# Expert products three steps apart, and three PSUM banks that change owner when the last transform ends

## The chip, the cores and the metric

One Trainium2 chip, one core of it. The metric is device time in microseconds (us) of one execution. The kernel before takes 2305.79 us, the median of three runs (2302.34 to 2326.87).

## The reference, cut to what matters

The input x has 8 sequences of 5696 tokens with 128 features. Every feature column is convolved causally with its own filter h (an FFT of twice the length, a product, the inverse FFT, the first 5696 outputs). The 45568 result rows then go through a mixture of eight experts, each token through one of them:

```
logits = y @ w_gate + modality_bias[modality_id];  e = argmax(logits);  g = softmax(logits)[e]
out[token] = g * (relu(y @ w1[e]) @ w2[e])          # w1: 128 x 1024, w2: 1024 x 128
```

All of it is float32. The kernel splits each factor of the expert products into a high and a low part and adds three products (high by high, low by high, high by low).

## The kernel before, in words

**Transform.** The convolution runs in stages with HBM between them: `stage1` and `stage23` for two groups of four sequences, then `stage4`, which ends the transform, computes the gate (logits, argmax, rank of each token in its expert) and sends each finished row by an indirect DMA of GpSimd to the region of its expert in HBM (`dispatch`, L298). The first 27 of 45 column blocks of `stage4` of the first group run beside `stage23` of the second group. All the rest of `stage4` runs beside the experts.

**Experts.** `Moe.run` works through 104 tiles in order: 81 tiles of 512 tokens and, at the end, 23 of 256 (`TSL`). A tile has eight steps, or four when it has 256 tokens. `gemm1` of step f multiplies one 128-wide slice of w1 with the tile's tokens (L567 to L569, three matmuls; six in a 256-token step, which does two slices), into one PSUM bank `ph`. ScalarE makes `hh`, the rectified high part (L572); VectorE then makes `hl`, the rest (L573), from `ph` and `hh`. `gemm2` of the same step takes `hh` and `hl` through a slice of w2 and adds into the bank `po` (L589 to L591; L589 needs only `hh`). It is issued `LAG` = 2 steps after `gemm1`.

Per tile there is also `load` (L535, the token rows by SP's queue, three tiles ahead), `load_weights` (L543, 2 MB into one of three slots, only where the expert of that slot changes), `prep` (L550, transposes of the tokens into a bank `pxt`, then `mxh` and `mxl`), and after the last `gemm2` the copy `ot` (L594), `finish` (L602, transposes back, into a bank of the same pool `pxt`; L605 scales by the gate) and `scatter` (L613, one indirect DMA of GpSimd per 128 tokens, one in each step). The calls hang on LAG: `load_weights` for tile t + 2 comes in step LAG - 1 of tile t, and `finish` of tile t - 1 in step LAG. `load` of tile t + 3 reuses the buffer of tile t - 2, so SP waits in it until the scatters of tile t - 2 have landed.

**PSUM.** There are eight banks: during the experts two for `ph`, two for `po`, one for `pxt`, and three for `stage4` (two `py`, one `pl`), held to the end of the kernel though `stage4` ends earlier.

**Order of the work.** SP's queue keeps the order in which the program issues. On the other engines a planner orders the instructions by a simulated timeline: each engine takes what is ready in the simulation, the earliest issued first. On the chip that order is fixed, and an engine that meets an instruction whose operands are not there waits. `run_all` (L712) issues steps of `rest()` (all that is left of the transform) and of `moe.run()` in turns.

Of the kernel before, what the change touches and what calls it, by code (L numbers as in the profile page):

```python
# [10 lines left out]
F32 = mybir.dt.float32  # L11
F32R = mybir.dt.float32r
# [13 lines left out]
TS = 512  # L26
# [39 lines left out]
def run_all(*gens):  # L66

    live = [[g, float(r), 0.0] for g, r in gens]
    while live:
        for it in list(live):  # L70
            it[2] += it[1]
            while it[2] >= 1.0:
                it[2] -= 1.0
                try:
                    next(it[0])
                except StopIteration:
                    live.remove(it)
                    break
# [3 lines left out]
def conv_moe(  # L82
# [436 lines left out]

    class Moe:  # L520
        def __init__(self, wp, sp, pst, psh, pso):
            self.sp, self.pst, self.psh, self.pso = sp, pst, psh, pso
            self.slots = [wp.tile([128, 2, 2, FF], F32R, name=f"slot{i}") for i in range(NSLOT)]
            self.st = {}
            self.outs = []
            self.tabs = {}

        def load(self, t):
            lv, j = JOBS[t]
# [15 lines left out]
        def prep(self, t):  # L545
            st = self.st[t]
            rt, ts, ns = st["rt"], st["ts"], st["ns"]
            px = self.pst.tile([128, NSUB, 128], F32, name="pxt")
            for c in range(ns):
                nc.tensor.transpose(px[:, c, :], rt[:, c, :D], ident)  # L550
            pf = px.rearrange("p c t -> p (c t)")[:, :ts]
            xh = self.sp.tile([128, TS], F32R, name="mxh")
            xl = self.sp.tile([128, TS], F32R, name="mxl")
            nc.scalar.copy(xh[:, :ts], pf)
            nc.vector.tensor_tensor(xl[:, :ts], pf, xh[:, :ts].bitcast(F32), op=ALU.subtract)
            st.update(xh=xh[:, :ts], xl=xl[:, :ts])

        def gemm1(self, t, f):
            w = self.slots[t % NSLOT]
            st = self.st[t]  # L560
            ts = st["ts"]
            n = TS // ts
            ph = self.psh.tile([128, TS], F32, name="ph")
            for i in range(n):
                fs = slice((f * n + i) * 128, (f * n + i + 1) * 128)
                po = ph[:, i * ts:(i + 1) * ts]
                nc.tensor.matmul(po, w[:, 0, 0, fs], st["xh"], start=True, stop=False)  # L567
                nc.tensor.matmul(po, w[:, 0, 0, fs], st["xl"], start=False, stop=False)  # L568
                nc.tensor.matmul(po, w[:, 0, 1, fs], st["xh"], start=False, stop=True)  # L569
            hh = self.sp.tile([128, TS], F32R, name="hh", bufs=4)  # L570
            hl = self.sp.tile([128, TS], F32R, name="hl", bufs=4)
            st["act"] = nc.scalar.activation(hh, ph, AF.Relu)  # L572
            nc.vector.scalar_tensor_tensor(hl, ph, 0.0, hh.bitcast(F32), op0=ALU.max, op1=ALU.subtract)  # L573
            st["h", f] = (hh, hl)
# [22 lines left out]
        def finish(self, t):  # L597
            st = self.st.pop(t)
            ns = st["ns"]
            pq = self.pst.tile([128, NSUB, 128], F32, name="pxt")  # L600
            for c in range(ns):
                nc.tensor.transpose(pq[:, c, :], st["ot"][:, c * 128:(c + 1) * 128], ident)  # L602
            of = self.sp.tile([128, NSUB, D], F32, name="of")
            rt = st["rt"]
            nc.vector.tensor_tensor(of[:, :ns], pq[:, :ns], rt[:, :ns, D:D + 1].to_broadcast([128, ns, D]), op=ALU.mult)  # L605
            ri = rt.bitcast(I32)
            for c in range(ns):
                self.outs.append((t, c, ri, of))
# [8 lines left out]
                    tc.add_manual_dep(d.ins, after.ins.name, PACED, reason="spacing")  # L617

        def run(self):
            LAG = 2  # L620
            total = len(JOBS)
            steps = []
            for t, (lv, j) in enumerate(JOBS):
                n = 4 if lv == len(LEVELS) - 1 else 8
                steps += [(t, f, n) for f in range(n)]
            self.load(0)
            self.load_weights(0)
            self.load(1)
            self.load_weights(1)
            self.load(2)  # L630
            self.prep(0)
            for g in range(len(steps) + LAG):
                t, f, n = steps[g] if g < len(steps) else (total, g - len(steps), 4)
                if f == 0 and t + 3 < total:
                    while JOBS[t + 3][0] not in self.tabs:
                        dispatch(4)
                        yield
                    self.load(t + 3)
                if t < total:
                    self.gemm1(t, f)  # L640
                    dispatch(1, self.st[t]["act"])
                    self.scatter(1, self.st[t]["act"])
                else:
                    self.scatter(1)
                if g >= LAG:
                    self.gemm2(*steps[g - LAG][:2])
                if f == LAG - 1 and t + 2 < total:
                    self.load_weights(t + 2)
                if t + 1 < total:
                    if f == (4 if n == 8 else 1):  # L650
                        self.prep(t + 1)
                if f == LAG and t >= 1:
                    self.finish(t - 1)
                yield
            if t < total or f < LAG:
                self.finish(total - 1)
            self.scatter(len(self.outs))
# [2 lines left out]
    ftab = fx.enter_context(tc.tile_pool(name="ftab", bufs=1, side="right")).tile([128, NQ, 2, 64], F32, name="ftab")  # L660
    with tc.tile_pool(name="s1a", bufs=2) as sp, tc.tile_pool(name="p1a", bufs=3, space=PSUM) as ps1:
        run_all((stage1(0, sp, ps1, ftab), 1))
    with tc.tile_pool(name="p4", bufs=2, space=PSUM) as ps4, \
            tc.tile_pool(name="p4l", bufs=1, space=PSUM) as ps4l:
        with tc.tile_pool(name="s2", bufs=2) as sp2, tc.tile_pool(name="p2x", bufs=3, space=PSUM) as psx, \
                tc.tile_pool(name="p2u", bufs=2, space=PSUM) as psu:
            with tc.tile_pool(name="s1b", bufs=2) as sp1:
                run_all((stage23(0, sp2, psx, psu), 3), (stage1(1, sp1, ps4, ftab), 2))
            fx.close()
            tp = ctx.enter_context(tc.tile_pool(name="table", bufs=1, side="right"))  # L670
            sp4 = ctx.enter_context(tc.tile_pool(name="s4", bufs=2, side="right"))
            with tc.tile_pool(name="ws", bufs=1) as wsp:
                run_all((stage23(1, sp2, psx, psu), 3), (stage4(0, sp4, ps4, ps4l, 0, QA, True), S4R), (presplit(wsp), 0.25))
            dispatch(len(queue))

        def fence():

            nc.gpsimd.dma_start(rows_d[E * REGION:E * REGION + TS, :].rearrange("(p c) w -> p c w", c=NSUB), padt)

        ev = [None] * (len(LEVELS) + 1)  # L680
        with tc.tile_pool(name="moew", bufs=1) as wp, tc.tile_pool(name="moe", bufs=2) as sp, \
                tc.tile_pool(name="pm1", bufs=1, space=PSUM) as pst, tc.tile_pool(name="pm3", bufs=2, space=PSUM) as psh, \
                tc.tile_pool(name="pm2", bufs=2, space=PSUM) as pso, tc.manual_schedule(engines={mybir.EngineType.SP}):
            moe = Moe(wp, sp, pst, psh, pso)

            def level(lv, src):
                tab, ev[lv] = table(tp, lv, ev[lv - 1])
                moe.tabs[lv] = (tab, src)

            s4 = stage4(0, sp4, ps4, ps4l, QA, NQ)  # L690
            for _ in range(AHEAD):
                next(s4)
            fence()
            level(0, views[NVIEW])

            def rest():
                yield from s4
                while queue:
                    yield
                fence()  # L700
                level(1, views[NVIEW])
                yield from stage4(1, sp4, ps4, ps4l, 0, NQ)
                while queue:
                    yield
                padrow = tp.tile([1, E], I32, name="padrow")
                nc.vector.tensor_copy(padrow, bases[0][0:1, :])
                for e in range(E):
                    r0 = nc.sync.value_load(padrow[0:1, e:e + 1], min_val=e * REGION, max_val=e * REGION + NTOK)
                    nc.sync.dma_start(rows_d[bass.ds(r0, TS), :].rearrange("(p c) w -> p c w", c=NSUB), padt)
                level(2, rows_d)  # L710
                level(3, rows_d)
            run_all((rest(), RATE), (moe.run(), 1))  # L712


# [81 lines left out]
```

## Time and profile before

| | |
|---|---|
| median of the runs shown | 2305.79 us |
| the profiled execution, its own time | 2318.76 us |
| its span, first to last instruction | 2317.0 us |
| TensorE (PE) busy | 2107.8 us, 91% |
| VectorE, ScalarE, GpSimd busy | 63%, 49%, 47% |
| mean granted clock of TensorE | 0.962 |

The span falls into stages: transform alone to about 870 us, transform and experts together to about 1595, experts alone with 512-token tiles to about 2130, with 256-token tiles to about 2305. Busy time of PE is modelled and short waits can be hidden in it, so the distance from the start of one matmul to the start of the next is read as well. The clock column is the share of full speed that the throttle granted.

### The profile page before, as it was taken

The page shows a single profiled execution, that of the slowest core. Times are in us where ns is not written, and L with a number is a line of the kernel's source. Part 1 is how long each engine was busy: PE and PEld are TensorE (multiplying, and loading weights), DVE is VectorE, ACT ScalarE, POOL GpSimd, SP SyncE. Part 2 cuts the span into 40 slices and gives each one's busy share as a digit, 9 for nine tenths or more (in the row PEclk, how much of TensorE's full clock was granted, in tenths as well). Part 3 has the DMA queues.
Part 4 walks back from the last instruction along what each step waited for, and adds up shares of the span by engine and source line. Part 5 has one row for each costly group of instructions (what it writes and reads, how often), then busy time and mean ns, then how long its engine had stood idle before and what let it go on. Part 6 is the DMA issues. An engine that isn't in the chain of part 4 may idle for free.

```text
span 2317.0 us, 33168 instructions
## 1 busy us (share of the span) xinstructions
PE 2107.8 (91%) x9598; PEld 1502.3 (65%) x9598; DVE 1466.0 (63%) x2473; ACT 1132.8 (49%) x2010; POOL 1085.6 (47%) x1050
## 2 busy tenths in 40 slices
PE   6779999899999897999899989889999999999997
PEld 5655555334444445777677667667888888888886
DVE  6559999776777984576465555555555555555443
ACT  6557776333333343555455555334444444444433
POOL 2126655344777763665665556553333333333222
PEclk9899999999999997999999999979999999999999
DMA  9999989899997765433244432132111121123331
GB/s 338 325 307 318 312 293 301 290 314 320 300 282 240 230 193 214 130 109 113 88 149 149 150 101 85 55 123 80 44 47 42 45 82 44 45 80 109 106 104 56
DMA packets 198309, 388.89 MB, mean 168 GB/s; under 512 B 32757, under 2 KB 63833, under 8 KB 193776
## 3 DMA queue, kind: packets, MB, share of 16 engines
q1 hardware_dynamic: 148832, 276.81, 36.5%
q10 hardware_dynamic: 25776, 62.34, 8.5%
q0 software_dynamic: 23520, 47.61, 6.2%
q8 instruction: 78, 1.28, 0.2%
q14 instruction: 103, 0.84, 0.1%
HBM read 393.95 MB, written 174.21 MB: 245 GB/s over the span
## 4 chain that ended last, share of the span: by engine, by line
PE 56%; issue 3%; ACT 2%; DVE 2%; another core or an unknown queue 2%; DMA 1%; POOL 1%; SPq 0%; POOLq 0%; ACTq 0%; DVEq 0%
PE ph L567 8%; PE ph L569 7%; PE po L589 7%; PE po L590 7%; PE po L591 7%; PE ph L568 7%; PE py L357 4%; PE pxt L602 2%; PE pxt L550 2%; PE py L364 1%; PE pl L371 1%; DVE hl L573 1%; ACT hh L572 1%; PE pu L239 1%
## 5 line engine op out<-in xcount | busy, mean ns | idle before, releaser
L573 DVE SCALAR_TENSOR_TENSOR hl<-ph,hh 128x512 fp32r<-128x512 f32 x740 | 506.7, 689 | 457.1 <-ACT hh L572 361.7
L572 ACT ACTIVATE hh<-ph 128x512 fp32r<-128x512 f32 x740 | 440.9, 599 | 600.0 <-PE ph L569 410.5
L613 POOL DMA_INDIRECT out<-of,mrt x370 | 363.1, 981 | 576.7 <-ACT hh L572 475.5
L298 POOL DMA_INDIRECT rows<-rt,idx x360 | 375.3, 1042 | 274.5 <-ACT hh L572 163.5
L271 POOL TENSOR_TENSOR t<-t,t 96x512 f32<-96x512 f32 x212 | 296.7, 1416 | 223.9 <-DVE t L264 214.4
L589 PE MATMUL po<-hh,slot 128*128 128x512 f32 (+1 forms) x832 | 328.3, 395 | 42.3 <-ACT hh L572 25.7
L264 DVE TENSOR_TENSOR t<-px,hs 96x512 f32<-96x512 f32 x512 | 318.2, 676 | 61.5 <-PE pu L239 17.4
L567 PE MATMUL ph<-mxh,slot 128*128 128x512 f32 (+1 forms) x832 | 331.1, 398 | 17.7 <-DVE hl L573 8.1
L590 PE MATMUL po<-hl,slot 128*128 128x512 f32 (+1 forms) x832 | 313.4, 377 | 0.1
L569 PE MATMUL ph<-mxh,slot 128*128 128x512 f32 (+1 forms) x832 | 312.1, 375 | 0.8 <-issue 0.8
L568 PE MATMUL ph<-mxl,slot 128*128 128x512 f32 (+1 forms) x832 | 312.7, 376 | 0.0
L591 PE MATMUL po<-hh,slot 128*128 128x512 f32 (+1 forms) x832 | 310.6, 373 | 0.0
L261 PE MATMUL px<-z,m 96*96 96x512 f32 x512 | 261.5, 610 | 11.1 <-DVE t L264 5.8
L589 PEld LDWEIGHTS po<-hh,slot 128*128 128x128 f32 x832 | 159.3, 192 | 82.4 <-ACT hh L572 36.5
L244 ACT COPY ut<-pu 90x512 f32<-90x512 f32 x256 | 145.0, 583 | 132.6 <-PE pu L239 60.3
L239 PE MATMUL pu<-t,mi 96*96 96x512 f32 x352 | 182.9, 625 | 20.7 <-ACT ut L244 11.4
L567 PEld LDWEIGHTS ph<-mxh,slot 128*128 128x128 f32 x832 | 159.7, 192 | 53.9 <-DVE hl L573 18.5
L590 PEld LDWEIGHTS po<-hl,slot 128*128 128x128 f32 x832 | 158.8, 191 | 35.5 <-DVE hl L573 2.7
L569 PEld LDWEIGHTS ph<-mxh,slot 128*128 128x128 f32 x832 | 159.1, 191 | 31.4 <-issue 0.5
L591 PEld LDWEIGHTS po<-hh,slot 128*128 128x128 f32 x832 | 158.7, 191 | 30.0
L568 PEld LDWEIGHTS ph<-mxl,slot 128*128 128x128 f32 x832 | 159.9, 192 | 23.6 <-issue 0.5
L261 PEld LDWEIGHTS px<-z,m 96*96 96x96 f32 x512 | 82.2, 166 | 115.4 <-issue 64.3
(157 smaller groups left out, 2892.2 us busy)
## 6 DMA issues: line engine op xcount, KB each, us to landing
slot<-w12s SPq DMA_DIRECT2D x104, 2048.0 KB
z<-z SPq DMA_DIRECT2D x256, 180.0 KB
z<-z SPq DMA_DIRECT2D x90, 320.0 KB
z<-z SPq DMA_DIRECT2D x90, 256.0 KB
ua<-ut SPq DMA_DIRECT2D x128, 180.0 KB
ub<-ut SPq DMA_DIRECT2D x128, 180.0 KB
mrt<-rows SPq DMA_DIRECT2D x81, 260.0 KB
w12s<-ws ACTq DMA_DIRECT2D x16, 1024.0 KB
```

Of the source, the lines that this page charges most:

```text
L261: nc.tensor.matmul(px[:KP], mm, zbuf[i][k % NZ], start=True, stop=True)
L264: nc.vector.tensor_tensor(prod[i, j].rearrange("p (b d) -> p b d", d=D), px[:KP].rearrange("p (b d) -> p b d", d=D), hs[:, j, k % KH].unsq ...
L298: d = nc.gpsimd.indirect_dma_start(views[count[0] % NVIEW], bass.IndirectOffsetOnAxis(ap=idx[:, t:t + 1], axis=0), rt[:, t, :], None, boun ...
L567: nc.tensor.matmul(po, w[:, 0, 0, fs], st["xh"], start=True, stop=False)
L568: nc.tensor.matmul(po, w[:, 0, 0, fs], st["xl"], start=False, stop=False)
L569: nc.tensor.matmul(po, w[:, 0, 1, fs], st["xh"], start=False, stop=True)
L572: st["act"] = nc.scalar.activation(hh, ph, AF.Relu)
L573: nc.vector.scalar_tensor_tensor(hl, ph, 0.0, hh.bitcast(F32), op0=ALU.max, op1=ALU.subtract)
L589: nc.tensor.matmul(po, w[:, 1, 0, fs], hh[:, cs], start=k == 0, stop=False)
L590: nc.tensor.matmul(po, w[:, 1, 0, fs], hl[:, cs], start=False, stop=False)
L591: nc.tensor.matmul(po, w[:, 1, 1, fs], hh[:, cs], start=False, stop=k == 7)
L613: d = nc.gpsimd.indirect_dma_start(oviews[(t * NSUB + c) % NVIEW], bass.IndirectOffsetOnAxis(ap=ri[:, c, D + 1:D + 2], axis=0), of[:, c, : ...
```

## The change

`LAG` goes from 2 to 3: `gemm2` is issued three steps after `gemm1`, and the calls that hang on LAG move one step later. `hh` and `hl` have five buffers instead of four. The PSUM pools of `stage4` move to the other end of PSUM, so that they can be closed alone. They are closed when `rest()` has issued its last work, and the three banks go to two new pools: from then on `ph` takes turns through four banks and `pxt` through two.

```diff
     class Moe:
         def __init__(self, wp, sp, pst, psh, pso):
-            self.sp, self.pst, self.psh, self.pso = sp, pst, psh, pso
+            self.sp, self.pst, self.psh, self.pso = sp, [pst], [psh] * 2, pso
+            self.n = [0, 0]
...
+        def bank(self, i, shape, name):
+            pools = (self.pst, self.psh)[i]
+            self.n[i] += 1
+            return pools[self.n[i] % len(pools)].tile(shape, F32, name=name)
...
-            px = self.pst.tile([128, NSUB, 128], F32, name="pxt")
+            px = self.bank(0, [128, NSUB, 128], "pxt")
...
-            ph = self.psh.tile([128, TS], F32, name="ph")
+            ph = self.bank(1, [128, TS], "ph")
...
-            hh = self.sp.tile([128, TS], F32R, name="hh", bufs=4)
-            hl = self.sp.tile([128, TS], F32R, name="hl", bufs=4)
+            hh = self.sp.tile([128, TS], F32R, name="hh", bufs=5)
+            hl = self.sp.tile([128, TS], F32R, name="hl", bufs=5)
...
-            pq = self.pst.tile([128, NSUB, 128], F32, name="pxt")
+            pq = self.bank(0, [128, NSUB, 128], "pxt")
...
-            LAG = 2
+            LAG = 3
...
-    with tc.tile_pool(name="p4", bufs=2, space=PSUM) as ps4, \
-            tc.tile_pool(name="p4l", bufs=1, space=PSUM) as ps4l:
+    px4 = ExitStack()
+    ps4 = px4.enter_context(tc.tile_pool(name="p4", bufs=2, space=PSUM, side="right"))
+    ps4l = px4.enter_context(tc.tile_pool(name="p4l", bufs=1, space=PSUM, side="right"))
+    with ExitStack() as late:
...
                 level(2, rows_d)
                 level(3, rows_d)
+                px4.close()
+                moe.psh = [psh] * 2 + [late.enter_context(tc.tile_pool(name="pm4", bufs=2, space=PSUM, side="right"))] * 2
+                moe.pst = [pst, late.enter_context(tc.tile_pool(name="pm5", bufs=1, space=PSUM, side="right"))]
```

## Rows read from the trace of the kernel before

**Rows 1.** The profile's page: the span, and busy time of PE.

```profile
span 2317.0 us, 33168 instructions
PE 2107.8 (91%) x9598; PEld 1502.3 (65%) x9598; DVE 1466.0 (63%) x2473; ACT 1132.8 (49%) x2010; POOL 1085.6 (47%) x1050
```

**Rows 2.** Busy time by stage (us from the span's start; then length, busy us and instructions of each engine, granted clock, busy share of the DMA engines, GB/s).

```profile
0.00:870.00 870.00, 766.83 (x2668) 420.78 (x2669) 677.69 (x996) 450.59 (x796) 460.80 (x409) 0.95 0.89 291
870.00:1595.00 725.00, 643.51 (x3249) 501.33 (x3248) 404.36 (x895) 352.84 (x634) 402.69 (x412) 0.94 0.38 122
1595.00:2130.00 535.00, 535.00 (x2475) 433.67 (x2474) 301.73 (x443) 258.31 (x443) 172.36 (x178) 1.00 0.18 56
2130.00:2152.00 22.00, 21.98 (x174) 21.09 (x172) 12.27 (x21) 10.63 (x21) 8.06 (x9) 1.00 0.41 138
2152.00:2297.40 145.40, 133.36 (x986) 119.20 (x987) 66.49 (x114) 57.24 (x113) 36.86 (x38) 1.00 0.30 101
```

**Rows 3.** Groups of PE instructions between 870 and 1595 us: the first matmuls of both expert products, with the idle time before them and what ended it.

```profile
L567 PE MATMUL ph<-mxh,slot 128*128 128x512 f32 x293 | 130.9, 447 | 14.0 <-DMA slot<-w12s 5.9 <-DVE hl L573 5.7 <-issue 1.8
L589 PE MATMUL po<-hh,slot 128*128 128x512 f32 x292 | 129.6, 445 | 42.3 <-ACT hh L572 25.7 <-issue 16.5
```

**Rows 4.** PE's waits between 900 and 1595 us: total, times, longest.

```profile
PE po L589 <- ACT hh L572: 25.7, 13, 4.9
PE po L589 <- issue: 16.5, 11, 4.2
PE ph L567 <- DVE hl L573: 5.7, 15, 1.2
```

**Rows 5.** PE in order of time around one such wait (start, duration, what, idle before).

```profile
1297.69 0.39 PE L591 MATMUL po<-hh,slot 128*128 128x512 f32 x1
1300.39 0.51 PE L589 MATMUL po<-hh,slot 128*128 128x512 f32 x1 [2.31 <-issue]
1301.12 0.59 PE L567 MATMUL ph<-mxh,slot 128*128 128x512 f32 x1 [0.22 <-DVE hl L573]
1301.50 0.63 PE L568 MATMUL ph<-mxl,slot 128*128 128x512 f32 x1
1301.93 0.63 PE L569 MATMUL ph<-mxh,slot 128*128 128x512 f32 x1
```

**Rows 6.** ScalarE, VectorE and GpSimd around the same wait.

```profile
1299.74 0.60 ACT L572 ACTIVATE hh<-ph 128x512 fp32r<-128x512 f32 x1 [5.51 <-remote]
1300.37 0.69 DVE L573 SCALAR_TENSOR_TENSOR hl<-ph,hh 128x512 fp32r<-128x512 f32 x1 [0.94 <-issue]
1296.42 0.98 POOL L613 DMA_INDIRECT out<-of,mrt  x1 [0.30 <-issue]
1297.70 0.97 POOL L298 DMA_INDIRECT rows<-rt,idx  x1 [0.30 <-issue]
```

**Rows 7.** The group of `gemm1`'s first matmul between 1595 and 2110 us.

```profile
L567 PE MATMUL ph<-mxh,slot 128*128 128x512 f32 x341 | 139.0, 408 | 0.0
```

**Rows 8.** Transposes of `finish` of two neighbouring 256-token tiles between 2130 and 2152 us, in order of time.

```profile
2142.44 0.38 PE L602 MATMUL pxt<-ident,ot 128*128 128x128 f32 x2
2148.52 0.38 PE L602 MATMUL pxt<-ident,ot 128*128 128x128 f32 x2
```

**Rows 9.** One 256-token tile after 2152 us, PE in order of time, from one `finish` to the next.

```profile
2182.53 0.44 PE L602 MATMUL pxt<-ident,ot 128*128 128x128 f32 x2 [0.46 <-ACT ot L594]
...
2184.10 0.28 PE L569 MATMUL ph<-mxh,slot 128*128 128x256 f32 x1
2184.36 0.39 PE L589 MATMUL po<-hh,slot 128*128 128x256 f32 x1
...
2185.09 0.38 PE L567 MATMUL ph<-mxh,slot 128*128 128x256 f32 x1
...
2189.49 0.28 PE L591 MATMUL po<-hh,slot 128*128 128x256 f32 x1
2190.23 0.44 PE L602 MATMUL pxt<-ident,ot 128*128 128x128 f32 x2 [0.46 <-ACT ot L594]
```

**Rows 10.** A weight load after 2152 us: the start of the tile in which it is issued, the issue, the stretch in which its traffic has ended, and the page's rows of DMA issues with their sizes.

```profile
2205.93 0.36 PE L567 MATMUL ph<-mxh,slot 128*128 128x256 f32 x1
2212.16 0.30 SPq L543 DMA_DIRECT2D slot<-w12s  x1
2219.00:2220.00 1.00, 1.00 (x8) 0.81 (x8) 0.94 (x2) 0.29 (x2) 0.70 (x1) 1.00 0.12 43
slot<-w12s SPq DMA_DIRECT2D x104, 2048.0 KB
mrt<-rows SPq DMA_DIRECT2D x23, 130.0 KB
```

**Rows 11.** `finish` (L602 on PE, L605 on VectorE) and the next `prep` (L550) of one tile in the shared stage, and L602 and L605 of another.

```profile
1327.51 0.60 PE L602 MATMUL pxt<-ident,ot 128*128 128x128 f32 x4
1328.69 0.69 DVE L605 TENSOR_TENSOR of<-pxt,mrt 128x512 f32<-128x512 f32 x1
1330.52 0.60 PE L550 MATMUL pxt<-ident,mrt 128*128 128x128 f32 x4
...
1280.95 0.66 PE L602 MATMUL pxt<-ident,ot 128*128 128x128 f32 x4
1286.32 0.68 DVE L605 TENSOR_TENSOR of<-pxt,mrt 128x512 f32<-128x512 f32 x1
```

## The prediction

> **What bounds the kernel now.** I read the page first: PE is busy for 91% of the span and no other engine comes near [rows 1]. That average covers stages with different limits, so the second view is busy time by stage [rows 2]. Before 870 us no expert step exists, and nothing of the change acts there. From 870 to 1595 us transform and experts share the chip: PE is idle for 725 - 643.5 = 81.5 us, at a mean granted clock of 0.94. From 1595 to 2130 us PE is busy for all 535 us at full clock. From 2152 to 2297 us, in the 256-token tiles, it is idle for 12 us and more is hidden in modelled ends.
>
> The third view says what ended PE's idle time in the shared stage. Before L589, the first matmul of the second product, it is 42.3 us; before L567, the first of the first product, 14.0, of which 5.9 is one wait for weights [rows 3]. L589 waits for `hh` (24 waits, 42.2 us, up to 4.9); L567 waits for `hl`, which is the release of its bank (15 waits, 5.7 us) [rows 4]. The fourth is the order of PE around one wait: L589 of step g - 2 stands first, then L567 to L569 of step g [rows 5]. ScalarE began `hh` only after 5.51 us of idle time that no engine of the profile ended, while GpSimd issued indirect DMAs one behind the other, 1.28 us apart [rows 6]. So the source of these waits is a late ScalarE, not a shortage of work on PE.
>
> The fifth view is the 256-token tiles: 6.08 us from one `finish` to the next at first [rows 8], then 7.70 us [rows 9]. After 2152 us PE drains between tiles: all of `gemm2` is done, `finish` waits for the copy `ot`, and only then the next tile's first product starts. 145.4 / 7.70 makes 19 such tiles.
>
> **The lag in the shared stage (870 to 1595 us).** There `ph` still has two banks, because the others come later. Call the late evacuation that of step g - 2. Before: PE stops at L589 of g - 2, which needs `hh`; one matmul later it stops again at L567 of g, which needs the bank, so `hl` of g - 2. After: L589 belongs to g - 3 and passes, and PE stops at L567 of g, for the same `hl`. In the wait shown, `hl` began at 1300.37 and took 0.69, and L567 started at 1301.12 [rows 5, 6]; it could start no earlier with a longer lag. What is queued behind the waiting L567 is what was queued behind it before: the rest of `gemm2` and the transform's matmuls. The matmul that used to run between the two waits now runs ahead of them. I take nothing for it. Bounds: if the planner puts all three matmuls of `gemm2` (0.7 us at the full clock) where they fill the wait, 24 x 0.7 = 17 us are gained; if PE instead idles where L589 used to run, 24 x 0.7 = 17 us are lost (1301.12 - 1300.39 = 0.73 each).
>
> **The lag in the 512-token tiles alone (1595 to 2130 us).** PE waits nowhere (0.0 us before 341 L567 [rows 7]), so neither lag nor banks have anything to remove: 0. The moved calls are covered: `load_weights` comes one step later, but the weights are used two tiles on, 14 steps. `finish` and its scatters move one step, and so does SP's `load`, which waits for those scatters; its rows are used more than two tiles later. A fifth buffer of `hh` and `hl` only keeps the distance that four gave. At the very end the drain has one more step of `gemm2` and the same matmuls: 0.
>
> **The 256-token tiles.** A drained tile costs 7.65 us (145.4 / 19) against 6.08 packed, 1.57 more. Part of it is the end: 2190.23 - 2189.49 = 0.74 from the last matmul to `finish`, where packed matmuls stand 0.12 apart, so 0.62. The other 0.95 is inside: after two steps of the first product the banks are full, L589 waits for `hh` (2184.10 to 2184.36), and the third step waits for `hl` (L567 at 2185.09) [rows 9]. With four banks all four steps of the first product can run behind each other, and with three steps between the products `hl` is ready before it is used. So 19 x 0.95 = 18.0 us go. The 0.62 stay as long as the planner puts `finish` ahead of the next tile, which it did before, when weights of the next tile were late in its simulation; the change makes them no earlier. If they went too, 19 x 1.57 = 29.8 us would be gained; if the order inside stays, 0.
>
> **What is late next: weights.** Each tile's second scatter now follows the second step of the tile after next, not the first, so one indirect DMA later: 1.28 us [rows 6]. SP waits in `load` for it, and `load_weights` stands behind `load` in SP's queue. Now the issue comes 6.2 us into the tile (2205.93, 2212.16), the traffic has ended between 2219 and 2220, and the weights are needed two tiles later, at 2205.93 + 2 x 7.70 = 2221.3: a slack of 1.3 to 2.3 us [rows 10], say 1.6. After, the issue is 1.28 later and the two tiles are 2 x 0.95 = 1.90 shorter; 3.18 - 1.6 = 1.6 us of waiting at L567 per load. Loads taken: 101 GB/s for 145.4 us is 14.7 MB; 19 tiles move some 0.26 MB each (130 KB of rows in, as much out), 5 MB; the rest is 4.7 loads of 2 MB, so 5. Cost 5 x 1.6 = 8.0 us, between 0 and 5 x 3.2 = 16.
>
> **Sum.** 0 + 0 - 18.0 + 8.0 = -10 us. The profiled execution took 2318.8 us (span 2317.0 and 1.8 around it), which gives 2309. It is 13 us above the median of 2305.8 but inside the spread of the runs shown; on the median the forecast is 2296 us. One per cent, 23 us, is about what a measurement of this kernel can tell from no change.
>
> **Rivals.** *The waits in the shared stage go too.* The 42 us before L589 are the largest wait that names a late expert operand; if the planner uses the longer lag to lay transform work in front of L567, they can be filled. Against it speaks that L567's bank is released no earlier. In full: 2306 - 10 - 42 = 2254 us, in half 2275, and a little less with a better clock. The Trainium skill (Perfetto Trace Analysis, Optimization Strategy) says that the same gap repeating on an engine that should be saturated can mean that SBUF or PSUM is too small for the next tile; by that rule the gaps at L589 would go with more buffers, and the sum would be the 2254 just worked out. The trace agrees only for the last 145 us: in the shared stage the gap ends with ScalarE, and the banks are given after it. Chance 0.18.
>
> *The tail keeps its order.* The planner still drains, L589 still stands behind two steps, and the later weights cost 5 x 1.28 = 6 us: 2306 to 2312 us. This is also the case in which the banks arrive where PE has no need of them. Chance 0.17.
>
> *Slower: `pxt` becomes the wait.* In the shared stage `pxt` keeps one bank. `finish` moves to the step right before `prep` of the next tile, which was two steps behind it: L602 at 1327.51, its read L605 over at 1329.38, L550 at 1330.52. A step less (1.5 us between the two L567 there) puts L550 at about 1329.0, 0.4 us too early; where VectorE is late, L605 ends 6.05 us after L602 [rows 11], and PE stands in L550 with the first product of the next steps behind it. For it: a bank that two users share at one step's distance. Against: an average step takes 725 / 293 = 2.5 us, and the planner sees the ordinary 1.9. There are 293 / 8 = 37 tiles; it decides if the mean wait exceeds (10 + 23) / 37 = 0.9 us, and at 1.5 us per tile it gives 2296 + 55 = 2351 us. Chance 0.13.
>
> **How the numbers follow.** The forecast has the remaining 0.52; its own range, from the bounds of the tail (29.8 gained and no weights late, to 18 gained and 16 given back) is 2276 to 2304. Faster by over 1% means under 2282.7: the first rival, and the lowest end of the forecast, 0.20. Slower by over 1% means over 2328.9: the last rival, 0.13. Within 1%: 0.67. The range that leaves out two in ten reaches from 2268, half of the first rival, to 2320, with the second rival and the loss bound of the shared stage less the tail's gain, and leaves out most of the last.
>
> **What would show it.** In the profile after: PE idle before L589 between 870 and 1595 us near zero and idle before L567 up by about as much; 1595 to 2130 us still 100% busy in the same length; from 2152 us on, twelve more matmuls of the first product behind each other before the first L589, a tile of about 6.7 us, `finish` still behind `ot`, and a handful of waits of L567 for weights. The prediction is wrong if the shared stage changes length by over 20 us, or if the tile stays at 7.7 us.

## The result, and the profile after

The changed kernel takes 2336.5 us (median of 19 runs, 2324.5 to 2347.4); the kernel before took 2318.2 beside them. The ratio is 1.0077 with an interval of 1.0057 to 1.0098: slower by 0.8%, some 18 us. The profiled execution took 2336.97 us with a span of 2335.2, so 18.2 more than the span before [rows 1]. Line numbers grow: L567, L572, L573, L589, L594, L602, L543 and L550 of before are L573, L578, L579, L595, L600, L608, L549 and L556 of after.

First the page's two lines: as many instructions on every engine as in [rows 1].

```profile
span 2335.2 us, 33122 instructions
PE 2111.2 (90%) x9598; PEld 1509.2 (65%) x9598; DVE 1437.8 (62%) x2473; ACT 1137.4 (49%) x2010; POOL 1070.3 (46%) x1050
```

Where the 18 us arise is read from the times at which stages begin and end. Below are groups of TensorE by line over the whole span (count, shortest, median and longest duration in ns, then the first and the last start in us): the two `stage1` (L180; `ps` is the first group of sequences, `py` the second), the filter matmuls of `stage23` (L222), and the first matmul of the experts' first product. Before:

```profile
L180 PE MATMUL ps<-xh,ft x360: 302/309/636, 8.0 to 144.1; 128*128 128x320 f32 x180
L180 PE MATMUL py<-xh,ft x180: 388/397/1415, 146.4 to 381.7; 128*128 128x512 f32 x180
L222 PE MATMUL pu<-hz,m x128: 377/379/457, 158.0 to 483.4; 96*96 96x256 f32 x128
L567 PE MATMUL ph<-mxh,slot x832: 277/397/796, 886.8 to 2301.6; 128*128 128x512 f32 x130, 128*128 128x256 f32 x37
```

After:

```profile
L180 PE MATMUL ps<-xh,ft x360: 302/309/636, 7.5 to 221.9; 128*128 128x320 f32 x180
L180 PE MATMUL py<-xh,ft x180: 388/396/628, 25.9 to 230.6; 128*128 128x512 f32 x180
L222 PE MATMUL pu<-hz,m x128: 378/379/740, 240.8 to 527.0; 96*96 96x256 f32 x128
L573 PE MATMUL ph<-mxh,slot x832: 277/394/796, 901.8 to 2317.5; 128*128 128x512 f32 x130, 128*128 128x256 f32 x37
```

The experts start at 901.8 instead of 886.8 us: 15.0 of the 18.2 us are lost before any expert step. The second group's `stage1` used to follow the first (146.4 against 144.1); now it starts at 25.9 and both end together at 230. `stage23` starts and ends later.

Busy time by stage tells what became of the early part (columns as in [rows 2]): before with the bounds 146, 484 and 870 us,

```profile
0.00:146.00 146.00, 102.67 (x540) 90.03 (x540) 87.17 (x105) 87.06 (x127) 19.52 (x45) 0.91 0.94 335
146.00:484.00 338.00, 306.92 (x964) 162.65 (x964) 292.34 (x361) 211.75 (x383) 190.37 (x146) 0.97 0.92 299
484.00:870.00 386.00, 357.24 (x1164) 168.10 (x1165) 298.19 (x531) 151.78 (x287) 250.91 (x218) 0.96 0.83 266
```

and after with the same events as bounds, then the shared stage, the 512-token tiles alone and the 256-token tiles:

```profile
0.00:231.00 231.00, 172.47 (x810) 137.11 (x810) 119.99 (x160) 167.57 (x280) 33.15 (x61) 0.95 0.99 359
231.00:527.00 296.00, 258.55 (x695) 116.40 (x695) 252.10 (x316) 141.33 (x240) 168.86 (x131) 0.91 0.88 284
527.00:885.00 358.00, 346.30 (x1165) 166.53 (x1164) 282.13 (x521) 144.44 (x275) 245.47 (x219) 0.98 0.78 240
885.00:1610.00 725.00, 639.56 (x3227) 502.36 (x3226) 402.16 (x892) 352.03 (x631) 400.09 (x411) 0.93 0.37 121
1610.00:2150.00 540.00, 540.00 (x2499) 438.05 (x2498) 299.92 (x447) 260.91 (x447) 171.41 (x177) 1.00 0.18 55
2150.00:2317.00 167.00, 149.72 (x1175) 144.59 (x1174) 78.51 (x134) 69.24 (x136) 45.66 (x48) 0.96 0.32 107
```

The two `stage1` side by side keep the DMA engines busy for 0.99 of 231 us while PE works 172 of them. `stage1` of the second group thereby costs 231 - 146 = 85 us; beside `stage23` it had cost 338 - 296 = 42. Of these 43 us, 28 come back in the third stretch (386 to 358). What has left that stretch is most of `presplit`, which splits the expert weights and moves 24 MB for it (16 loads of 512 KB, 16 writes of 1 MB). Its loads and its writes, first and last issue, before:

```profile
L450 ACTq DMA_DIRECT2D ws<-in_w x16: 346/352/385, 391.3 to 651.7; - x16
L453 ACTq DMA_DIRECT2D w12s<-ws x16: 338/339/381, 402.4 to 660.3; - x16
```

After:

```profile
L450 ACTq DMA_DIRECT2D ws<-in_w x16: 346/346/383, 242.7 to 502.0; - x16
L453 ACTq DMA_DIRECT2D w12s<-ws x16: 338/338/368, 251.4 to 511.3; - x16
```

The third stretch moves 358 x 240 instead of 386 x 266, so 86 MB instead of 103. That this gives the 28 us back is argued: no run moved `presplit` alone.

In the shared stage the waits are these (total, times, longest, as [rows 4]):

```profile
PE po L595 <- ACT hh L578: 23.2, 13, 4.2
PE ph L573 <- DVE hl L579: 9.4, 10, 3.7
PE po L595 <- issue: 6.4, 4, 2.9
PE ph L573 <- DMA slot<-w12s: 6.1, 1, 6.1
```

And in the 256-token tiles, from 2150 to 2320 us:

```profile
PE ph L573 <- DMA slot<-w12s: 9.5, 5, 2.7
PE pxt L608 <- ACT ot L600: 7.5, 16, 0.5
```

One tile there, PE in order of time, answers to [rows 9]; behind it the same engine at a tile whose weights came late.

```profile
2180.38 0.44 PE L608 MATMUL pxt<-ident,ot 128*128 128x128 f32 x2 [0.52 <-ACT ot L600]
2180.58 0.36 PE L573 MATMUL ph<-mxh,slot 128*128 128x256 f32 x1
...
2183.36 0.28 PE L575 MATMUL ph<-mxh,slot 128*128 128x256 f32 x1
...
2183.61 0.36 PE L595 MATMUL po<-hh,slot 128*128 128x256 f32 x1
...
2187.18 0.44 PE L608 MATMUL pxt<-ident,ot 128*128 128x128 f32 x2 [0.46 <-ACT ot L600]
...
2238.90 0.44 PE L608 MATMUL pxt<-ident,ot 128*128 128x128 f32 x2 [0.46 <-ACT ot L600]
2241.90 0.55 PE L573 MATMUL ph<-mxh,slot 128*128 128x256 f32 x1 [2.56 <-DMA slot<-w12s]
```

All 24 matmuls of the first product (2180.58 to 2183.36) now run ahead of the second, and the tile takes 6.80 us instead of 7.70. But five times PE stands for weights, and with the three longest of these waits (1.96, 2.56 and 2.73 us) the granted clock falls to 0.50, the lower of its two levels (1.2 and 2.4 GHz), and stays there for 2 to 6 us; with the other two (0.94 and 1.30) it stays at 1.00. The first row holds such a wait and what follows, the second a tile without a wait (the same columns as the stages):

```profile
2239.00:2248.00 9.00, 6.44 (x33) 6.23 (x34) 2.50 (x4) 2.40 (x5) 1.93 (x2) 0.62 0.26 97
2264.00:2271.00 7.00, 6.54 (x54) 6.12 (x53) 3.52 (x6) 3.03 (x6) 1.94 (x2) 1.00 0.81 291
```

From its start to the end of the span this part takes 184.8 us (2150.4 to 2335.2) where it took 185.0 (2132.0 to 2317.0). With the shared stage and the 512-token tiles 3.4 us longer together (901.8 to 2150.4 against 886.8 to 2132.0), the sum is 15.0 + 3.4 - 0.2 = 18.2.

### The profile page after: what moved, and what is told of

Read it like the earlier page. It is cut to its first block, busy times and chain, and to the rows that moved or that the text cites. A ratio compares the mean times of both kernels' runs of the same rounds, so it can differ in the third digit from the quotient of the medians.

```text
span 2335.2 us, 33122 instructions
## 1 busy us (share of the span) xinstructions
PE 2111.2 (90%) x9598; PEld 1509.2 (65%) x9598; DVE 1437.8 (62%) x2473; ACT 1137.4 (49%) x2010; POOL 1070.3 (46%) x1050
## 5 line engine op out<-in xcount | busy, mean ns | idle before, releaser
L579 DVE SCALAR_TENSOR_TENSOR hl<-ph,hh 128x512 fp32r<-128x512 f32 x740 | 506.8, 689 | 383.6 <-ACT hh L578 324.9
L578 ACT ACTIVATE hh<-ph 128x512 fp32r<-128x512 f32 x740 | 440.4, 599 | 566.7 <-PE ph L575 398.8
L298 POOL DMA_INDIRECT rows<-rt,idx x360 | 367.7, 1022 | 285.9 <-ACT hh L578 171.4
L271 POOL TENSOR_TENSOR t<-t,t 96x512 f32<-96x512 f32 x212 | 289.9, 1384 | 177.7 <-DVE t L264 168.9
L595 PE MATMUL po<-hh,slot 128*128 128x512 f32 (+1 forms) x832 | 321.0, 386 | 32.1 <-ACT hh L578 23.2
L573 PE MATMUL ph<-mxh,slot 128*128 128x512 f32 (+1 forms) x832 | 325.5, 391 | 26.6 <-DMA slot<-w12s 15.5
L596 PE MATMUL po<-hl,slot 128*128 128x512 f32 (+1 forms) x832 | 321.3, 386 | 0.4 <-DVE hl L579 0.2
L597 PE MATMUL po<-hh,slot 128*128 128x512 f32 (+1 forms) x832 | 310.9, 374 | 0.0
L261 PE MATMUL px<-z,m 96*96 96x512 f32 x512 | 269.8, 625 | 8.6 <-DMA z<-z 4.3
L244 ACT COPY ut<-pu 90x512 f32<-90x512 f32 x256 | 144.1, 581 | 161.4 <-PE pu L239 84.5
L595 PEld LDWEIGHTS po<-hh,slot 128*128 128x128 f32 x832 | 159.9, 192 | 68.8 <-ACT hh L578 29.8
L573 PEld LDWEIGHTS ph<-mxh,slot 128*128 128x128 f32 x832 | 161.8, 195 | 61.1 <-issue 18.4
L239 PE MATMUL pu<-t,mi 96*96 96x512 f32 x352 | 178.0, 609 | 7.5 <-ACT hs L224 3.4
L575 PEld LDWEIGHTS ph<-mxh,slot 128*128 128x128 f32 x832 | 161.9, 195 | 30.5
L574 PEld LDWEIGHTS ph<-mxl,slot 128*128 128x128 f32 x832 | 162.2, 195 | 25.9
```

The source lines that it names most:

```text
L261: nc.tensor.matmul(px[:KP], mm, zbuf[i][k % NZ], start=True, stop=True)
L298: d = nc.gpsimd.indirect_dma_start(views[count[0] % NVIEW], bass.IndirectOffsetOnAxis(ap=idx[:, t:t + 1], axis=0), rt[:, t, :], None, boun ...
L595: nc.tensor.matmul(po, w[:, 1, 0, fs], hh[:, cs], start=k == 0, stop=False)
L596: nc.tensor.matmul(po, w[:, 1, 0, fs], hl[:, cs], start=False, stop=False)
L597: nc.tensor.matmul(po, w[:, 1, 1, fs], hh[:, cs], start=False, stop=k == 7)
```

## The experiments

The theory that this profile suggests: **early order**. `stage1` of the second group takes its PSUM banks from `stage4`'s `py` pool. At its old end this pool began in banks of the first `stage1`, so the second had to wait for the first; at the other end its two banks are free from the start, and the planner lays the two beside each other. The rival: the loss comes from the **lag** and what hangs on it. Each ratio below is to the kernel before on the same chip. Beside the first four it took 2306.8 us, beside runs 5 to 8 2218.0, beside 9 to 11 2219.6, beside run 12 2304.9 in one execution (more on this at the end).

**1. The place of `stage4`'s pools alone.**

```diff
-    with tc.tile_pool(name="p4", bufs=2, space=PSUM) as ps4, \
-            tc.tile_pool(name="p4l", bufs=1, space=PSUM) as ps4l:
+    with tc.tile_pool(name="p4", bufs=2, space=PSUM, side="right") as ps4, \
+            tc.tile_pool(name="p4l", bufs=1, space=PSUM, side="right") as ps4l:
```

> The kernel before with one thing changed: the PSUM pools of stage4 (two py banks, one pl bank) lie at the other end of PSUM. LAG 2, four buffers of hh and hl, no handover. Theory early: the banks that stage1 of the second group uses are then other banks than those of stage1 of the first group, the two run side by side, stage23 starts at 233 us instead of 152, and the first matmul of the experts comes at 902 us instead of 887; the time is 13 to 18 us above the kernel before (ratio 1.006 to 1.008). Rival lag: the loss of the changed kernel comes from the longer lag and the later weights, so this kernel is within 3 us of the kernel before and its first expert matmul stands at 887 us.

Measured: 1.0095 (1.007 to 1.012), a little above what the theory gave. The same groups as above:

```profile
L180 PE MATMUL py<-xh,ft x180: 387/396/628, 26.0 to 231.8; 128*128 128x512 f32 x180
L567 PE MATMUL ph<-mxh,slot x832: 277/397/796, 902.0 to 2305.1; 128*128 128x512 f32 x130, 128*128 128x256 f32 x37
```

The place of the pools alone brings the whole loss, and the experts start at 902.0.

**2. The changed kernel with the old early order.** `stage4`'s pools stay where they were, the experts' pools go to the other end.

```diff
-    ps4 = px4.enter_context(tc.tile_pool(name="p4", bufs=2, space=PSUM, side="right"))
+    ps4 = px4.enter_context(tc.tile_pool(name="p4", bufs=2, space=PSUM))
... (p4l in the same way)
-                tc.tile_pool(name="pm1", bufs=1, space=PSUM) as pst, tc.tile_pool(name="pm3", bufs=2, space=PSUM) as psh, \
+                tc.tile_pool(name="pm1", bufs=1, space=PSUM, side="right") as pst, tc.tile_pool(name="pm3", bufs=2, space=PSUM, side="right") as psh, \
... (pm2 in the same way; pm4 and pm5 go the other way)
```

> The changed kernel, but stage4's PSUM pools stay where they were, and the experts' pools lie at the other end of PSUM instead, so that the handover is still possible. LAG 3, five buffers and the handover as in the changed kernel. Theory early: stage1 and stage23 are ordered as in the kernel before, first expert matmul at 887 us, and what remains of the loss is the 4 us of the shared stage and nothing of the 256-token tail: the time is within 5 us of the kernel before (ratio 0.998 to 1.002). Rival lag: the loss stays, 15 us or more above the kernel before (ratio 1.0065 or more).

Measured: 0.9988 (0.9968 to 1.0009). Lag, buffers and handover together are worth nothing that can be measured; the lag as the cause of the loss falls.

**3. The handover without the longer lag**: run 2 with LAG 2 and four buffers.

```diff
... (hh and hl: bufs=4)
-            LAG = 3
+            LAG = 2
```

> As the run before it (stage4's pools where they were, handover of three banks), but LAG 2 and four buffers of hh and hl: the handover alone. Theory banks: the four ph banks alone take the inner gaps out of the 256-token tiles, and with LAG 2 the scatters, and so the weights, come one step earlier than with LAG 3, so of the 9.5 us of waits for weights in the tail at most 4 are left: tail 8 to 15 us shorter than the 185 us of both kernels, the time 5 to 15 us below the kernel before. Rival lag needed: with two steps between the products L595 still waits for hh inside the tile, the tail is 180 to 185 us, and the time within 4 us of the kernel before.

Measured: 0.996 (0.994 to 0.998), 2296.4 us; the tail takes 176.4 us from its first matmul (2109.9) to the end (2286.3). PE's waits for weights there are 5.3 us in five, more than the 4 expected, where run 2 has 8.0 in four. A tile between them takes 6.8 us as in the changed kernel (`finish` at 2187.27 and 2194.06). The four banks are enough to take the inner gaps out; the third step of lag isn't needed for it and makes the weights later.

**4. Weights ahead of rows**: run 2, in the 256-token tiles with another order in SP's queue.

```diff
                 if f == 0 and t + 3 < total:
...
-                    self.load(t + 3)
+                    if n == 8:
+                        self.load(t + 3)
...
                 if f == LAG - 1 and t + 2 < total:
                     self.load_weights(t + 2)
+                if f == LAG - 1 and n == 4 and t + 3 < total:
+                    self.load(t + 3)
```

> As the second run (stage4's pools where they were, LAG 3, handover), and in the 256-token tiles the load of the token rows of tile t + 3 is issued after the weights of tile t + 2 instead of two steps ahead of them, so the weights no longer stand behind rows that wait for scatters. Theory weights: the 9.5 us of waits for weights and the two stretches at half clock behind them (some 7 us) go; tail 165 to 170 us instead of 185, the time 12 to 20 us below the second run; if the planner also packs the tiles again (6.0 us each instead of 6.8), another 15 us. Rival slot: the weights wait for their slot, which the last second product of tile t - 1 frees, and not for SP's queue; tail 180 us or more, time within 4 us of the second run.

Measured: 0.9898 (0.9867 to 0.993), 2279.9 us. All of PE's waits in the tail up to the last first product, and the row of that stretch, which here runs at the full clock:

```profile
PE pxt L608 <- ACT ot L600: 4.7, 10, 0.5
PE po L596 <- DVE hl L579: 0.5, 1, 0.5
```

```profile
2108.90:2256.10 147.20, 141.93 (x1179) 139.24 (x1178) 77.10 (x136) 69.29 (x137) 46.57 (x49) 1.00 0.36 121
```

Run 2 took 165.3 us for that stretch, at 0.96 of the clock:

```profile
2119.50:2284.80 165.30, 149.73 (x1178) 144.96 (x1177) 79.11 (x135) 69.28 (x137) 46.08 (x48) 0.96 0.32 108
```

No wait for weights is left, so the weights did stand behind the rows in SP's queue and not for their slot. To the end of the span the tail takes 164.0 us, run 2's 183.0. The time is 24.9 us below run 2, more than the first part of the theory gave; 7.2 us of that lie in the profiles before the first expert matmul (879.2 against 886.4).

**5. The smallest cure of the order**: the changed kernel, and the pool of the first `stage1` goes to the other end too.

```diff
-    with tc.tile_pool(name="s1a", bufs=2) as sp, tc.tile_pool(name="p1a", bufs=3, space=PSUM) as ps1:
+    with tc.tile_pool(name="s1a", bufs=2) as sp, tc.tile_pool(name="p1a", bufs=3, space=PSUM, side="right") as ps1:
```

> The changed kernel with one thing more: the pool of stage1 of the first group (six banks) also lies at the other end of PSUM, so that stage4's pools, from which stage1 of the second group takes its banks, again share banks with it. stage23 uses the same banks as in the changed kernel. Theory order: the loss comes from the two stage1 standing side by side and goes when they can't; stage23 starts at 152 to 158 us, the first expert matmul comes at 880 to 890 us, the time is that of the second run (ratio to the kernel before 0.996 to 1.002). Rival place: what costs is the place of stage23's banks or of stage4's, and the ratio stays at 1.006 or more.

Measured: 0.9991 (0.9973 to 1.0008).

```profile
L180 PE MATMUL py<-xh,ft x180: 387/397/1061, 149.8 to 384.9; 128*128 128x512 f32 x180
L573 PE MATMUL ph<-mxh,slot x832: 277/394/765, 887.2 to 2197.5; 128*128 128x512 f32 x130, 128*128 128x256 f32 x37
```

With `stage4`'s and `stage23`'s banks where the changed kernel has them, the loss is gone as soon as the two `stage1` share banks again. It is the order, and not the place of these banks.

**6. The lag alone**: the kernel before with LAG 3 and five buffers.

```diff
... (hh and hl: bufs=5)
-            LAG = 2
+            LAG = 3
```

> The kernel before with LAG 3 and five buffers of hh and hl, no pool touched. Theory neutral: in the shared stage the waits of the second product get less (20 us instead of 42) and others take their place, so the shared stage keeps its length; in the tail two ph banks keep the inner gaps, the weights come about 1.3 us later than before, at 7.7 us a tile still almost in time: ratio 1.000 to 1.003. Rival lag gains: the longer lag shortens the shared stage by 10 us or more, ratio 0.996 or less. Rival lag costs: weights late five times at 2 to 3 us and a clock drop behind each, ratio 1.005 or more.

Measured: 1.0021 (1.0005 to 1.0036), as the first theory has it. In the tail PE waits 4.1 us in four for weights, and the tail takes 190.9 us (2033.2 to 2224.1). The shared stage's part of the expectation couldn't be seen: no wait for `hh` occurs there at all (last section).

**7 and 8. Weights first with LAG 2**, with the handover (run 3 with the edit of run 4) and without it (the kernel before with that edit alone).

> The third run (stage4's pools where they were, LAG 2, four buffers, handover) with the weights of tile t + 2 issued ahead of the rows of tile t + 3 in the 256-token tiles. Theory weights: the 5.3 us of waits for weights that the third run has left go, and what follows them; the tail is 160 to 166 us as in the fourth run, the time 10 to 20 us below the third run (ratio to the kernel before 0.987 to 0.992). Rival lag needed: with weights in time the two-step lag lets L595 wait for hh, tail 170 us or more, ratio 0.993 or more.

> The kernel before with the weights of tile t + 2 issued ahead of the rows of tile t + 3 in the 256-token tiles, and nothing else: LAG 2, two ph banks to the end. Theory both needed: the planner packs the tiles (it sees the weights in time), but with two ph banks the inner gaps stay in part; tail 165 to 178 us, ratio 0.992 to 0.997. Rival weights alone: the tail is as short as in the fourth run, 160 to 165 us, and the four banks were never needed, ratio 0.988 to 0.991. Rival banks: the tail stays at 182 to 185 us, ratio 0.998 to 1.002.

Measured: 0.991 (0.9887 to 0.9933) with the handover, tail 163.1 us (2036.8 to 2199.9); 0.9928 (0.9902 to 0.9953) without it, tail 167.0 (2027.4 to 2194.4). The order in SP's queue alone gives most of it: the planner then packs the tiles, and one takes 6.78 us with two `ph` banks too (`finish` at 2098.80 and 2105.58 in run 8). Two `ph` banks keep small waits for the bank in the tail:

```profile
PE ph L567 <- DVE hl L573: 5.8, 17, 0.3
```

With four banks these are gone and the tail is about 4 us shorter; the two ratios' intervals overlap.

**9 and 10. Why is the early order dear? VectorE.** Every second `yl` of `stage23` goes to GpSimd, in the changed kernel (9) and in run 5 (10).

```diff
-            nc.vector.tensor_tensor(yl, y, yh.bitcast(F32), op=ALU.subtract)
+            (nc.gpsimd if k % 2 else nc.vector).tensor_tensor(yl, y, yh.bitcast(F32), op=ALU.subtract)
... (low is handed k)
```

> The changed kernel, in which every second subtraction that makes yl (L231, 1.8 us each, 40 in all, all in stage23 of the first group) runs on GpSimd instead of VectorE: some 36 us less of VectorE in that stage. It tells why the two stage1 side by side cost time. Theory VectorE: the stage that is left without stage1 beside it (231 to 527 us) is bound by VectorE, and is 15 us or more shorter here; the time is 10 us or more below the changed kernel. Rival chain: that stage is bound by its chain of loads, products and copies, and the same subtraction on GpSimd, which takes longer for one, leaves its length within 5 us or makes it longer.

> The fifth run (the two stage1 one behind the other again) with the same subtractions on GpSimd. If VectorE bounds stage23 there too, with stage1 of the second group beside it, 155 to 489 us gets shorter by 10 us or more; if that stretch is bound by the transfers of both (0.93 of the DMA engines' time), it stays within 5 us.

**11. The changed kernel once more**, beside these two.

> The changed kernel as it is, beside the two others and the kernel before on the same chip: ratio 1.005 to 1.010, first expert matmul at 902 us. If the chip shows no waits of the second product for hh, as in the fifth to the eighth run, the shared stage has the length of the fifth run.

Measured: 1.0057 (1.0026 to 1.0088) for 9, 0.9963 (0.9936 to 0.999) for 10, 1.0072 (1.0041 to 1.0103) for 11. The loss of the change is there again, though the first expert matmul came at 895.4 and not at 902 us. The stretch of `stage23` from its first matmul to the last L222 is 518.1 - 228.7 = 289.4 us in 9 and 523.4 - 230.8 = 292.6 in 11, though VectorE worked less in it:

```profile
231.00:520.00 289.00, 256.84 (x696) 116.41 (x697) 229.96 (x299) 141.26 (x241) 220.90 (x144) 0.92 0.89 288
```

```profile
231.00:527.00 296.00, 262.99 (x702) 115.19 (x703) 256.59 (x322) 142.68 (x242) 170.51 (x125) 0.92 0.88 283
```

Over the stage's own bounds VectorE works 228.1 us in 9 and 253.0 in 11: 25 us less of VectorE, 3 us less of time. VectorE doesn't bound that stage, and the rival of this run holds in so far. In 10 the stretch kept its length too (152.7 to 488.8, against 155.2 to 488.5 in run 5). Run 10's ratio lies clear below 1, and its experts start at 880.2 us instead of 887.2; but runs 3 and 4, without this edit, start them at 877.8 and 879.2, so a gain by it isn't shown. From the first expert matmul to the tail, 11 takes 1144.8 us (895.4 to 2040.2) and run 5 1147.0 (887.2 to 2034.2), so there too the change costs nothing after the early stages. In the nine traces in which the second `stage1` follows the first (before, runs 2 to 8 and 10) the first expert matmul comes at 877.8 to 887.2 us; in the five with the two side by side (after, runs 1, 9, 11 and 12) it comes at 890.8 to 902.0.

**12. The transfers.** The changed kernel with most loads of `stage23` of the first group left out.

```diff
-            if k < K1:
+            if k < K1 and (g == 1 or k < NZ):
                 for i in range(2):
                     nc.sync.dma_start(zbuf[i][k % NZ][:90], zd[g][i][:, k, :GC])
```

> The changed kernel, in which stage23 of the first group loads only the first 4 of its 64 pairs of z blocks and works on with these: 120 loads of 180 KB are left out, 22 MB of the 84 MB that move between 231 and 527 us (296 us at 283 GB/s). The convolution of the first group is so computed from other data; the amount of work on every engine is the same. Only the length of the early stages is read. Theory transfers: the stretch of stage23 that is left without stage1 beside it is bound by transfers and is 40 us or more shorter. Rival chain: it is bound by the chain of matmul, product and copy inside a step and stays within 10 us of the 293 us from its first matmul to the last of L222 in the changed kernel.

Measured: 234.0 to 522.2 us, so 288.2 against 293.5 in the profile after (233.5 to 527.0).

```profile
231.00:527.00 296.00, 263.35 (x705) 118.95 (x706) 254.68 (x324) 142.66 (x243) 182.76 (x132) 0.91 0.66 213
```

The DMA engines' share falls from 0.88 to 0.66 and the stage stays within 5.3 us. So `stage23` without `stage1` beside it is bound neither by transfers of this size nor by VectorE. It isn't alone there: `presplit` runs beside it in the profile after and in runs 9, 11 and 12. The chain of matmul, product and copy inside a step is one candidate that is left. TensorE's own work is another: over the stage's own bounds PE is busy for 258.5 of 293.5 us after and for 257.0 of 289.4, 259.5 of 292.6 and 258.6 of 288.2 in runs 9, 11 and 12, at a clock of 0.91 or 0.92, more than any other engine. Nothing was tried that tells the two apart.

## Why the prediction was wrong

It gave 2296 us with a range of 2268 to 2320; 2336.5 lies above it. Of the 40 us between, 12.4 are the kernel before itself, which took 2318.2 beside these runs; with the ratio on the 2305.8 that the prediction started from, the time would be 2323.6, still outside. The other 28 are, in the two profiles, 15.0 before the experts, 3.4 up to the tail, and a tail of -0.2 where -10 was forecast.

**The step that failed** is the first: "Before 870 us no expert step exists, and nothing of the change acts there." The diff moves the pools of `stage4`, and the code that the prediction had before it says who else uses them: `stage1(1, sp1, ps4, ftab)`. Giving that pool banks of its own took away a wait, and with it an order that was good. Run 1 shows that this alone brings the loss, runs 2 and 5 that nothing is left of it without. It is worth 15.0 us in the two profiles. What makes the new order dear is read from the rows and not tested: beside `stage23` the second `stage1` costs 42 us; beside the first one, where transfers already take 0.94 of the DMA engines' time, 85. The Trainium skill (Perfetto Trace Analysis, Optimization Strategy) says that a kernel whose most contended engine changes over time may gain from interleaving such regimes; these runs agree, in the reverse: the interleaving was there, and 0.7 to 0.95% went with it (the result, runs 1 and 11).

**The lag in the shared stage: 0, between -17 and +17.** The size holds: from the first expert matmul to the start of the tail the profile after has 3.4 us more, and the lag alone costs 0.2% in all (run 6, where these waits don't occur), its late weights in the tail with it. What was to be seen came only in part: idle time before L595 fell from 42.3 [rows 3] to 32.1 instead of to zero, and L573's wait for `hl` rose from 5.7 [rows 4] to 9.4. The part that names `hh` hardly changed, 25.7 to 23.2; what fell is the part that names nothing, 16.5 to 6.4. In the other traces that have such waits it is 30.9 and 35.5 us with LAG 2 (runs 1 and 3) and 20.7, 22.3 and 25.0 with LAG 3 (runs 2, 4 and 12). So "L589 belongs to g - 3 and passes" is wrong for most of these waits. One cause is at hand, though argued: ScalarE's idle time that no engine ended is up to 6.7 us long in the profile after, and an average step takes 2.5.

**The 512-token tiles: 0.** Held: 540 us, 100% busy at full clock.

**The tail's gaps: -18.0.** The mechanism held: 24 matmuls of the first product in front, `finish` still behind `ot`, 6.80 us for a tile where 6.7 was predicted. That it takes the lag besides the banks was wrong: run 3 has the gain with LAG 2, and run 8 has such a tile with LAG 2 and two banks, once the weights are in time for the planner.

**Weights late: +8.0, in five waits.** Measured 9.5, in five. What the term left out is what comes with a wait: at three of the five the granted clock falls from 1.00 to 0.50 for a while (0.62 on the mean between 2239 and 2248 us, with a wait of 2.56). The mean over the 167 us is 0.96 where [rows 2] have 1.00, so 0.04 x 167 = 6.7 us more. And the drain at the very end, taken as 0, grew from 15.4 to 17.7 us (from the last first product to the end of the span). So the tail's sum was -18.0 + 9.5 + 6.7 + 2.3 = +0.5 instead of -10, measured -0.2: all that the banks won went to the weights.

**The rivals.** *The waits in the shared stage go too* fell: they went by a quarter. The rule of the Trainium skill named there (Perfetto Trace Analysis, Optimization Strategy), that a gap repeating on the engine that should be saturated can mean too few buffers, holds in the tail, where four banks took the inner gaps out, and not in the shared stage, where in runs 5 to 8 the waits were 0.0 with two banks as well, in 7 and 8 also with four buffers of `hh`. *The tail keeps its order* fell with the 6.80 us. *`pxt` becomes the wait* fell: L556 waited 1.8 us in three for VectorE between 900 and 1600 us, and the loss has another cause. No rival had the early stages; the chance of 0.67 for a difference within 1% was met for a reason that the prediction didn't know.

**A version that beats both**: run 4 (the changed kernel without the move of `stage4`'s pools, weights first) and run 7 (LAG 2) are 1.0% and 0.9% below the kernel before.

## What to carry to other kernels

A buffer pool is also an order: before moving one, list every stage that takes tiles from it, and ask which wait its old neighbours enforced and whether that wait kept two stages with the same bound apart. When a gap is closed ahead of a queue with little slack, price the next thing in the queue first; here a change of the order of two calls, weights ahead of rows, was worth 0.7% (run 8) while lag, buffers and banks together gave nothing that could be measured (run 2). A short wait of TensorE costs more than its length if the granted clock falls with it: here 9.5 us of waits and 6.7 us more.

## What the runs showed that was not expected

The waits of the second product for `hh`, on which much of the prediction's text rests, aren't a property of the kernel. Beside runs 5 to 8 the kernel before took 2218.0 us instead of 2306.8, and in the traces of runs 5 to 11 the shared stage has none of them. Between 870 and 1595 us, the kernel before with LAG 3 (run 6), to be held against [rows 2, 3]:

```profile
870.00:1595.00 725.00, 698.85 (x3705) 565.61 (x3704) 459.59 (x977) 402.38 (x715) 435.60 (x445) 0.98 0.39 128
```

```profile
L589 PE MATMUL po<-hh,slot 128*128 128x512 f32 x357 | 147.6, 415 | 0.0
```

In the same 725 us PE issues 3705 instructions there (3697 in run 8, with LAG 2) instead of 3249, while the early stages keep their length (first expert matmul at 886.6 us, before 886.8). The single instructions are no slower: between 900 and 1590 us one `hh` takes 600 ns before and 599 in run 6, one indirect DMA of `dispatch` 1021 and 1019 on GpSimd. What differs is idle time of ScalarE and VectorE that ended with an event of no engine and no queue of this core (`remote`). Before, between 870 and 1595 us (total, times, longest):

```profile
ACT hh L572 <- remote: 47.5, 13, 6.6
```

All seven traces with the waits for `hh` (before, after, runs 1 to 4 and 12) have such idle time between 870 and 1610 us, 23.1 to 47.5 us before `hh` alone; the seven of runs 5 to 11 have none. It doesn't go by the chip's number, which is 1 on record for runs 1 to 4 and for 9 to 11. Where these events come from stays open; it was not tried. The ratios are not touched by it: the changed kernel gave 1.0077 beside the one and 1.0072 beside the other.
